# One order for attention and experts: a place for every buffer, attention scores in four row tiles, layer 1 of the first group beside attention

## The chip, the cores and the metric

One core of one Trainium2 chip. The metric is device microseconds of one execution, the median of several runs of the same program. The kernel is written by hand against the five engines: TensorE (PE), VectorE (DVE), ScalarE (ACT), GpSimd (POOL) and SyncE (SP), which issues all DMAs from one queue.

## What is computed

A chunked linear attention with decay, then two expert layers without routing, one after the other, on 3072 tokens.

```python
# attention: x (4, 8, 768, 32), a (4, 8, 768), B and C (4, 8, 768, 16); per chunk:
cum = np.cumsum(log(clip(a)), axis=-1)
L = np.exp(cum[:, :, :, None] - cum[:, :, None, :]) * causal
y = einsum('bhij,bhjd->bhid', einsum('bhin,bhjn->bhij', C, B) * L, x)
y += einsum('bhin,bhnd->bhid', C, state) * np.exp(cum)[..., None]
state = decay_full * state + sum_j B_j x_j * decay_from_j
# layer 1: (3072, 256) -> 768 -> 256
h = np.maximum(np.maximum(x @ w1, x @ w2), x @ w3);  y = h @ w_out
# layer 2: (3072, 256) -> 2048 -> 256
h = y @ w_in
P = a0 + a1*h + a2*h**2 + a3*h**3;  Q = 1 + abs(b0)*abs(h) + abs(b1)*h**2
out = (P / (Q + 1e-6)) @ w_out
```

The expert weights arrive as 64-bit floats and are converted on the chip.

## The kernel before

**Tiling.** The sequence is cut into NG = 6 groups of 128 positions of all 4 batches, so a group has T = 512 columns. A group has NU = 8 units u (a batch and a half of the 8 heads). Tensors of a unit or of a group are 128 x 512 floats; one such tile in PSUM is one of eight banks.

**Attention, per unit** (lines 585 to 642). `d_mm(u)` forms the 128 x 512 differences of the cumulated logarithms in a bank (tile `d`): two matmuls, in group 0 the second in fp32 on a tile `tl` that DVE builds. ACT takes the exponential into `e`. `s_mm(u)` forms the scores of two units at once (tile `s`): K is 64 (4 heads x 16 states), so the array holds two row tiles side by side, and the C operand `cz` is laid out block-diagonally, four heads to a unit, most of it zeros. `m_op(u)` (DVE) multiplies `s` by `e` into `m`, `y_intra(u)` multiplies by the values in four column tiles. Per group there are `y_inter` (state times C), `state` (a matmul into a `d` bank, masked and summed by DVE), `prep` (a matmul into a `d` bank, an exponential, a POOL multiplication) and `y_out` (ACT copies two banks; from group 1 on they go to DRAM, `xt_d`, and come back later as `xst`).

**Banks of attention.** `pd` holds 2 banks (`d`), `psc` 4 (`s`, two pairs), `py` 2 (`y`).

**Experts.** All expert matmuls are three fp32r passes (`mm3`, lines 768 to 770: high by high, low by high, high by low). `gy_plan(g)` is layer 1 of a group: for each of 6 slices f three blocks of 6 matmuls with ACT and DVE taking the running maximum `xa`, then the split into `hhi` (ACT) and `hlo` (POOL), then 72 matmuls into two banks: 144 x 512 columns in all. `h_plan` and `o_plan` are layer 2: per group 16 slices with 6 + 6 matmuls, and between them the rational function on ACT, DVE and POOL. In the last group `o` is a single fp32 matmul each. Layer 2 of group g is interleaved with layer 1 of group g+1; layer 1 of group 0 stands alone.

**Weights.** `plan_conv` brings in a piece (512 KB: 256 x 256 64-bit numbers) by DMA into one of 3 `wraw` buffers and converts it: two ACT operations and three DVE operations (lines 364, 367, 370) into `wa` and `we`, two POOL additions (375), an ACT copy to the high part (377 by way of 313), two POOL subtractions (379) to the low part. 28 pieces: 9 of `w1`, `w2`, `w3`, 3 of `wo1`, 8 of `win`, 8 of `wo2`.

**Order.** Each step is recorded with its engine, a cost and a due time; a planner (`Plan.emit`) finds a start for every step by list scheduling in some rounds and writes the steps out in that order, so that each engine has a fixed queue. Steps have a phase: attention is phase 0, the experts and the `wo2` pieces are phase 1, the other weight pieces have none. All of phase 0 is written before any of phase 1, and between the two `second()` closes the buffers of attention (SBUF and PSUM) and opens those of the experts, which lie on the same memory.

Of the kernel before, what the change touches and what calls it, by code (L numbers as in the profile page):

```python
# [21 lines left out]
CH = 128  # L22
# [12 lines left out]
LEAD = 3  # L35
# [10 lines left out]
class _Tile:  # L46
    def __init__(self, make, prev=None, before=None, given=None):
        self.make, self.prev, self.before, self.t = make, prev, before, given
        self.given = given is not None
        self.first, self.writers, self.readers, self.closed = -1 if self.given else None, [], [], False  # L50


class _Op:
# [3 lines left out]
    def __init__(self, i, engine, busy, fn, first, deps, after, at, phase, lock, mode, size):  # L57
        self.i, self.engine, self.busy, self.fn, self.first = i, engine, busy, fn, first
        self.deps, self.after, self.at, self.phase = deps, after, at, phase
        self.lock, self.mode, self.size = lock, mode, size  # L60
        self.plain = busy + (Plan.SWITCH if mode in ("s", "d", "ya", "st") else 0.0)
# [33 lines left out]
class Plan:  # L95
# [5 lines left out]
    ROUNDS, LOOK = 6, (0.0, 0.1, 0.2)  # L101

    def __init__(self):
        self.ops, self.rings, self.phase = [], {}, 0

    def tile(self, ring, size, make):
        ts = self.rings.setdefault(ring, [])
        t = _Tile(make, ts[-size] if len(ts) >= size else None, ts[-1] if ts else None)
        ts.append(t)
        return t  # L110

    def op(self, engine, busy, fn, reads=(), writes=(), at=None, behind=(), lock=False, mode="", size=0.0):
        i = len(self.ops)
        deps, after = set(), {w for t in behind for w in t.writers}
        for t in reads:
            assert (t.writers or t.given) and not t.closed
            deps.update(t.writers)
            t.readers.append(i)
        for t in writes:
            assert not t.closed  # L120
            if t.first is None:
                t.first = i
                if t.before and not t.before.given:
                    after.add(t.before.first)
                if t.prev:
                    t.prev.closed = True
                    deps.update(t.prev.writers + t.prev.readers)
# [5 lines left out]
                            self.phase, lock, mode, size))  # L133

    def listed(self, key, look):
# [6 lines left out]
        ready, start, end = {}, [0.0] * (n + 1), [0.0] * (n + 1)  # L142
        held = {"pool": 0.0, "dve": 0.0}
        moved, mode, landed = 0.0, "", [0.0] * self.FLIGHTS

        def at(j):
            t = self.BEGIN
            for i, _ in self.before[j]:
                if i == n or i in ops[j].after:
# [7 lines left out]
        def can(j):  # L157
            if j == n:
                start[n] = max(start[i] for i, _ in self.before[n])
                done(n)  # L160
            else:
                ready[j] = at(j)
                wait[ops[j].engine].append(j)

        def done(i):
            for j, _ in self.then[i]:
                left[j] -= 1
                if not left[j]:
                    can(j)

        for j in [j for j in range(n) if not left[j]]:
            can(j)
        for _ in range(n):
            t, e = min((max(free[e], min(ready[j] for j in w)), e) for e, w in wait.items() if w)
            j = min((j for j in wait[e] if ready[j] <= t + look), key=lambda j: (key[j], j))
            wait[e].remove(j)
            t, o = max(t, ready[j]), ops[j]
# [16 lines left out]
            done(j)  # L194
        return start, max(end)

    def placed(self, key, before, then, begin):

        n = len(before)
# [5 lines left out]
        while heap:  # L205
            _, j = heapq.heappop(heap)
            t = begin
            for i, l in before[j]:
                t = max(t, start[i] + l)
            if j < len(self.ops):  # L210
                o, last = self.ops[j], None
                while t != last:
                    last = t
                    for r in o.uses:
                        t = lines.setdefault(r, _Line()).fit(t, o.plain)
                for r in o.uses:
                    lines[r].take(t, o.plain)
# [7 lines left out]
    def emit(self, second):  # L225

        ops, n = self.ops, len(self.ops)
        self.before, self.then = [[] for _ in range(n + 1)], [[] for _ in range(n + 1)]

        def edge(i, j, l):  # L230
            self.before[j].append((i, l))
            self.then[i].append((j, l))

        for o in ops:
            for i in o.deps:
                edge(i, o.i, ops[i].lag(o))
            for i in o.after:
                edge(i, o.i, 0.0)
            if o.phase == 0:
                edge(o.i, n, 0.0)  # L240
            elif o.phase == 1:
                edge(n, o.i, 0.0)
        span = [o.plain for o in ops] + [0.0]
        back = [[(j, l - span[i] + span[j]) for j, l in self.then[i]] for i in range(n + 1)]
        key = [0.0] * (n + 1)
        for i in reversed(range(n)):
            key[i] = min([1e9 if ops[i].at is None else ops[i].at] +
                         [key[j] - l for j, l in self.then[i] if j < n])
        best = None
        for _ in range(self.ROUNDS):  # L250
            for look in self.LOOK:
                start, end = self.listed(key, look)
                if best is None or end < best[0]:
                    best = end, start
            start = best[1]
            mirror = self.placed([-(start[i] + span[i]) for i in range(n + 1)], back, self.before, 0.0)
            far = max(mirror[i] + span[i] for i in range(n + 1))
            key = [far - mirror[i] - span[i] for i in range(n + 1)]
        start = best[1]
        order = sorted(range(n), key=lambda i: (start[i], i))  # L260
        last = max(k for k, i in enumerate(order) if ops[i].phase == 0)
        early = [i for i in order[:last + 1] if ops[i].phase != 1]
        late = [i for i in order[:last + 1] if ops[i].phase == 1] + order[last + 1:]
        for part in (early, late):
            if part is late:
                second()
            for i in part:
                for t in ops[i].first:
                    t.t = t.make()
                ops[i].fn()  # L270
# [3 lines left out]
def decay_attention_max_moe_rational_moe(  # L274
# [23 lines left out]
    cvr = ctx.enter_context(tc.tile_pool(name="cvr", bufs=3))  # L298
    cva = ctx.enter_context(tc.tile_pool(name="cva", bufs=2))
    cve = ctx.enter_context(tc.tile_pool(name="cve", bufs=2))  # L300
    mp1 = ctx.enter_context(tc.tile_pool(name="mp1", bufs=1))
# [15 lines left out]
    def split(o_hi, o_lo, src, e_lo):  # L317
        copy(act, o_hi, src)
        e_lo.tensor_tensor(out=o_lo, in0=src, in1=o_hi.bitcast(F32), op=ALU.subtract)

    wsb = {}

    def w_alloc(nm, k, n, pl=wp):
        wsb[nm] = [
            pl.tile([128, k, n], F32R, name=f"{nm}_{s}") for s in ("hi", "lo")
        ]
# [3 lines left out]
    def plan_conv(plan, tok, nm, src, k0, c0):  # L330

        if nm == "wo2":
            hi, lo = (lambda i=i: wsb[nm, k0 // 2][i] for i in range(2))
        else:
            hi, lo = (lambda i=i: wsb[nm][i][:, k0:k0 + 2, c0:c0 + 256] for i in range(2))
        shape = [128, 2, 256]
        wide = src.dtype != F32
        raw = plan.tile("wraw", 3, lambda: cvr.tile(shape + [2], U32, tag="wraw", name="wraw") if wide
                        else cvr.tile(shape, F32, tag="wraw", name="wst"))
        rows = slice(128 * k0, 128 * k0 + 256)  # L340
        if not wide:
            plan.op("dma", 0.4, lambda: nc.sync.dma_start(
                out=raw.t, in_=src[rows, c0:c0 + 256].rearrange("(k p) n -> p k n", p=128)), [], [raw], size=262.0)
            plan.op("act", 0.53, lambda: copy(act, hi(), raw.t), [raw], [tok])
            plan.op("pool", 1.26, lambda: pool.tensor_tensor(out=lo(), in0=raw.t, in1=hi().bitcast(F32),
                                                             op=ALU.subtract), [raw], [tok])
            return
        a = plan.tile("wa", 2, lambda: cva.tile(shape, U32, tag="wa", name="wa"))
        e = plan.tile("we", 2, lambda: cve.tile(shape, U32, tag="we", name="we"))
        af = lambda: a.t.bitcast(F32)  # L350
        low, high = (lambda: raw.t[:, :, :, 0]), (lambda: raw.t[:, :, :, 1])
        raws[0] += 1
        first = f"w{raws[0]}" in FIRST
# [4 lines left out]
        plan.op("dma", 0.42, lambda: nc.sync.dma_start(  # L358
            out=raw.t.rearrange("p k n t -> p k (n t)"),
            in_=src.bitcast(U32)[rows, 2 * c0:2 * c0 + 512].rearrange("(k p) n -> p k n", p=128)), [], [raw],  # L360
            FIRST.index(f"w{raws[0]}") - 1000.0 if first else 6.0 + PIECE * raws[0],
# [725 lines left out]
```

## Time and profile before

| | us |
|---|---|
| median of 3 runs (lowest to highest) | 576.49 (576.09 to 577.17) |
| the profiled execution | 576.76 |
| its span, first to last instruction | 575.0 |
| busy: PE / DVE / ACT / POOL | 555.9 / 512.4 / 439.6 / 439.9 |

A profile is one execution. Matmuls are pipelined: a matmul of 512 columns is shown as 389 ns, while the next starts 225 ns after it, so rates are read from start to start, not from the mean. Waits are inferred; the engine named is the one whose event came last.

### The profile page before, as it was taken

What the parts mean: (1) busy time and instruction counts of PE and PEld (TensorE: products, weight loads), DVE (VectorE), ACT (ScalarE), POOL (GpSimd) and SP (SyncE); (2) the same over time, 40 slices, a digit from 0 to 9 for tenths busy, and PEclk for the clock granted to TensorE, in tenths of its full rate; (3) what the DMA queues carried; (4) which work ended last, traced back from release to release, by engine and by line L of the source; (5) the groups of instructions that cost most, each with busy time, mean ns of one, the idle gap of its engine ahead of it and who ended that gap; (6) DMA issues with size and microseconds to landing.
All of it is one profiled execution on the core that took longest, in us unless ns stands there. A gap on an engine that the chain in (4) does not pass through costs nothing.

```text
span 575.0 us, 8132 instructions
## 1 busy us (share of the span) xinstructions
PE 555.9 (97%) x2758; PEld 410.0 (71%) x2758; DVE 512.4 (89%) x777; ACT 439.6 (76%) x756; POOL 439.9 (77%) x410
## 2 busy tenths in 40 slices
PE   8998889899999999999999999999999999999997
PEld 3333333678788888888888888888888888887563
DVE  7998978689999998889888988898898888988996
ACT  5787767576888878787878787878777868688993
POOL 1787767798999777768587877676866999869883
PEclk9999999999999999999999999999999999999999
DMA  7878873542000100101000000000000010001000
GB/s 213 265 213 303 261 223 112 198 132 73 1 0 2 33 5 0 38 1 38 0 1 36 1 20 19 0 26 12 1 1 2 0 38 0 1 1 38 1 0 36
DMA packets 19044, 33.70 MB, mean 59 GB/s; under 512 B 3523, under 2 KB 4027, under 8 KB 19003
## 3 DMA queue, kind: packets, MB, share of 16 engines
q1 hardware_dynamic: 19003, 33.20, 18.1%
q8 instruction: 21, 0.34, 0.2%
q14 instruction: 20, 0.16, 0.1%
HBM read 27.27 MB, written 5.91 MB: 58 GB/s over the span
## 4 chain that ended last, share of the span: by engine, by line
PE 70%; DVE 11%; POOL 9%; DMA 4%; ACT 3%; issue 2%; SPq 1%; POOLq 0%; ACTq 0%; DVEq 0%
PE pg L768 9%; PE pg L770 9%; PE pg L769 9%; PE ph L770 6%; PE ph L769 6%; PE ph L768 6%; PE po L770 6%; PE po L769 6%; PE po L768 6%; DVE m L627 2%; PE s L594 2%; DVE wa L370 2%; PE po L990 1%; POOL wa L375 1%; DVE wa L364 1%
## 5 line engine op out<-in xcount | busy, mean ns | idle before, releaser
L972 POOL TENSOR_TENSOR glo<-w,ghi 128x512 fp32r<-128x512 f32 x80 | 106.3, 1329 | 21.6 <-ACT ghi L313 21.3
L768 PE MATMUL pg<-xhi,w_hi 128*128 128x512 f32 x202 | 79.3, 392 | 1.7 <-DVE xa L851 1.4
L769 PE MATMUL pg<-xlo,w_hi 128*128 128x512 f32 x202 | 78.6, 389 | 0.0
L770 PE MATMUL pg<-xhi,w_lo 128*128 128x512 f32 x202 | 78.6, 389 | 0.0
L959 ACT ACTIVATE pr<-v,qc 128x512 f32<-128x512 f32 x83 | 57.4, 692 | 18.7 <-POOL v L938 11.5
L313 ACT ACTIVATE ghi<-w 128x512 fp32r<-128x512 f32 x80 | 50.5, 631 | 23.3 <-PE po L770 20.0
L412 POOL TENSOR_TENSOR hlo<-xa,hhi 128x512 fp32r<-128x512 f32 x36 | 49.7, 1383 | 20.5 <-ACT hhi L313 20.5
L770 PE MATMUL ph<-yhi,win_lo 128*128 128x512 f32 x160 | 62.2, 389 | 0.0
L768 PE MATMUL ph<-yhi,win_hi 128*128 128x512 f32 x160 | 62.2, 389 | 0.0
L769 PE MATMUL ph<-ylo,win_hi 128*128 128x512 f32 x160 | 62.2, 389 | 0.0
L768 PE MATMUL po<-ghi,wo_hi 128*128 128x512 f32 x160 | 62.2, 389 | 0.0
L769 PE MATMUL po<-glo,wo_hi 128*128 128x512 f32 x160 | 62.2, 389 | 0.0
L770 PE MATMUL po<-ghi,wo_lo 128*128 128x512 f32 x160 | 62.2, 389 | 0.0
L964 DVE SCALAR_TENSOR_TENSOR pr<-w,co,pr 128x512 f32<-128x512 f32 x83 | 62.1, 749 | 0.0
L938 POOL TENSOR_TENSOR v<-t,v 128x512 f32<-128x512 f32 x44 | 57.2, 1299 | 3.6
L961 DVE SCALAR_TENSOR_TENSOR v<-v,pr 128x512 f32<-128x512 f32 x83 | 56.4, 680 | 3.6 <-ACT pr L960 3.2
L375 POOL TENSOR_TENSOR wa<-wa,we 128x256 uint32<-128x256 uint32 x56 | 44.8, 814 | 19.1 <-DVE wa L370 17.7
L966 DVE SCALAR_TENSOR_TENSOR w<-v,pr 128x512 f32<-128x512 f32 x83 | 56.7, 684 | 1.8
L960 ACT ACTIVATE pr<-pr 128x512 f32<-128x512 f32 x86 | 50.2, 584 | 1.6
L851 DVE TENSOR_TENSOR xa<-xa,pg 128x512 f32<-128x512 f32 x67 | 45.6, 681 | 4.4 <-PE ph L770 2.1
L768 PEld LDWEIGHTS pg<-xhi,w_hi 128*128 128x128 f32 x202 | 37.9, 188 | 11.5 <-DVE xa L851 2.2
L956 POOL TENSOR_TENSOR w<-w,t 128x512 f32<-128x512 f32 x20 | 25.9, 1296 | 24.3 <-DVE v L945 22.2
(167 smaller groups left out, 1475.2 us busy)
## 6 DMA issues: line engine op xcount, KB each, us to landing
wraw<-in_wo_dram SPq DMA_DIRECT2D x11, 512.0 KB
wraw<-in_w_dram SPq DMA_DIRECT2D x9, 512.0 KB
wraw<-in_win_dram SPq DMA_DIRECT2D x8, 512.0 KB
xn<-in_xn_dram SPq DMA_DIRECT2D x6, 512.0 KB
out_dram<-ob SPq DMA_DIRECT2D x12, 256.0 KB
xt_d<-xo SPq DMA_DIRECT2D x10, 256.0 KB
xst<-xt_d SPq DMA_DIRECT2D x10, 256.0 KB
bt<-in_bz_dram SPq DMA_DIRECT2D x6, 256.0 KB
```

Source lines behind the costliest of these rows:

```text
L313: act.activation(out=o, in_=i, func=AF.Copy)
L375: plan.op("pool", 0.7, lambda k=k: pool.tensor_tensor(out=a.t[:, k], in0=a.t[:, k], in1=e.t[:, k], op=ALU.add), [e], [a])
L768: pe.matmul(dst, wh, hi, start=first, stop=False)
L769: pe.matmul(dst, wh, lo, start=False, stop=False)
L770: pe.matmul(dst, wl, hi, start=False, stop=last)
L938: pop(1.26, lambda: pool.tensor_tensor(out=f(v), in0=f(t1), in1=f(v), op=ALU.mult), [t1], [v])
L959: aop(0.6, lambda: act.activation(out=f(r), in_=f(v), func=AF.Ln, bias=qc), [v], [r])
L960: aop(0.49, lambda: act.activation(out=f(r), in_=f(r), func=AF.Exp, scale=-1.0), [], [r])
L961: dop(0.6, lambda: dve.scalar_tensor_tensor(out=f(v), in0=f(v), scalar=QC, in1=f(r), op0=ALU.add, op1=ALU.mult), [r], [v])
L964: dop(0.67, lambda: dve.scalar_tensor_tensor(out=f(r), in0=f(w), scalar=c(0), in1=f(r), op0=ALU.add, op1=ALU.mult), [w], [r])
L966: dop(0.6, lambda: dve.scalar_tensor_tensor(out=f(w), in0=f(v), scalar=2.0, in1=f(r), op0=ALU.subtract, op1=ALU.mult), [v, r], [w])
L972: pop(1.26, lambda: pool.tensor_tensor(out=f(lo), in0=f(w), in1=f(hi).bitcast(F32), op=ALU.subtract), [w, hi], [lo])
```

## The change

- **One plan.** The phases and `second()` are gone, and with them the rule that all of attention is written before any expert step. The planner gets one more choice (`KEEP`: prefer a PE step of the same tiling mode for up to 1.5 us), 8 rounds instead of 6.
- **A place for each buffer.** Instead of pools that are closed and opened there is one SBUF pool and one PSUM pool in which each tile names its place, and a tile waits for the last tile of that place, whatever it was. The eight banks are S0 to S3, D, G, Y0, Y1. Attention: scores in S0 to S3, `y` in Y0 and Y1, and `d`, `prep` and `state` all in D (in group 0 alone every other `d` is in G). Experts: `pg` = G, D; `ph` = S0, S1; `pr` = Y0, Y1; sums in S2, S3. Layer 1 of group 0 (18 + 2 banks, `EARLY` = 20) uses G alone. The eight `wo2` weight pairs lie where `cz`, `lr`, `xn` and `xo` of attention lay.
- **Scores as four row tiles.** K is 32 (2 heads x 16 states); one `s_mm` now does half a group: two batches x four row tiles, each 256 columns, into four banks. `cz` is half as large. Heads are regrouped accordingly in the host layout of B, C and `a`. There are 12 `s_mm` instead of 24, and each needs all four S banks free of the one before.
- **Coarser steps.** `y_intra` does two units in one step (24 steps instead of 48), `y_inter` all batches in one, `y_out` writes one 512 KB transfer, and `x_plan` reads one.
- **Layer 1 of group 0** can lie beside attention; its six `hlo` subtractions go to DVE instead of POOL.
- **Weights on the host** are laid out so that each piece is one run of 4 KB per partition (two of 2 KB before).

```diff
-    ROUNDS, LOOK = 6, (0.0, 0.1, 0.2)
+    ROUNDS, LOOK, KEEP = 8, (0.0, 0.1, 0.2), (0.0, 1.5)
-    def tile(self, ring, size, make):
-        ts = self.rings.setdefault(ring, [])
-        t = _Tile(make, ts[-size] if len(ts) >= size else None, ts[-1] if ts else None)
+    def tile(self, place, make):
+        t = _Tile(make, self.last.get(place, ()))
+        self.last[place] = [t]
         return t
...
-        early = [i for i in order[:last + 1] if ops[i].phase != 1]
-        late = [i for i in order[:last + 1] if ops[i].phase == 1] + order[last + 1:]
-        for part in (early, late):
-            if part is late:
-                second()
+        for i in best[1]:
...
-    cz = [sp.tile([128, 4, T], F32, name=f"cz{i}") for i in range(2)]
+    cz = [sl.tile([128, 2, T], F32, tag=f"L{i}", name=f"cz{i}") for i in range(2)]
...
-    def s_mm(u):
-        s_t[u], s_t[u + 1] = ts = new("psc", "s", 4), new("psc", "s", 4)
+    def s_mm(k):
+        ts = [bank(f"S{h}") for h in range(4)]
         def mm():
-            for q, t in enumerate(ts):
-                r = slice(64 * q, 64 * q + 64)
-                pe.matmul(t.t.rearrange("p (f i) -> p f i", f=4), btg[g].t[r, c], cz[g % 2][r, :, c],
-                          start=True, stop=True)
+            for b in range(2):
+                c = slice(CH * (2 * a + b), CH * (2 * a + b) + CH)
+                for h, t in enumerate(ts):
+                    r = slice(32 * h, 32 * h + 32)
+                    pe.matmul(t.t.rearrange("p (h b i) -> p h b i", h=2, b=2)[:, :, b], btg[g].t[r, c],
+                              cz[g % 2][r, :, c], start=(b == 0), stop=True, skip_group_check=True)
...
     def d_mm(u):
-        t = new("pd", "d", 2)
+        t = bank("G" if g < PAIR and d_n[0] % 2 else "D")
...
     def state(g):
-        t = new("pd", "d", 2)
+        t = bank("D")
...
+    for k in range(F2 // 2):
+        wsb["wo2", k] = new(f"L{(0, 1, 6, 7, 2, 3, 4, 5)[k]}", (128, 2, 2, DM), F32R)
...
+    pg, ph, pr = (ring(p, bank) for p in (["G", "D"], ["S0", "S1"], ["Y0", "Y1"]))
     def gy_bank(g):
-        if g == 0 and banks[0] % 5 > 2:
-            return new("ph", "ph", 2)
-        return new("pg", "pg", 2)
+        if g:
+            return pg()
+        return bank("G") if banks[0] <= EARLY else late()
...
-            psplit(of(xa), hi, lo, "pool")
+            psplit(of(xa), hi, lo, "pool" if g else "dve")
```

## Rows read from the trace of the kernel before

**Rows 1.** Windows: stretch, length, busy of each engine (instructions), granted clock, DMA share, GB/s

```profile
0.00:10.00 10.00, 7.71 (x25) 3.21 (x25) 7.74 (x16) 5.36 (x10) 2.04 (x6) 1.00 0.65 188
10.00:103.60 93.60, 82.71 (x741) 33.96 (x739) 83.89 (x139) 66.88 (x121) 66.27 (x79) 0.98 0.72 224
103.60:139.60 36.00, 34.93 (x155) 28.04 (x152) 29.17 (x37) 22.45 (x40) 30.93 (x34) 1.00 0.48 161
139.60:215.40 75.80, 75.17 (x330) 61.59 (x329) 73.57 (x108) 62.54 (x108) 64.38 (x58) 1.00 0.03 8
215.40:291.20 75.80, 75.80 (x336) 62.77 (x335) 67.97 (x104) 59.82 (x102) 55.62 (x47) 1.00 0.04 14
```

**Rows 2.** Timeline of PE in attention: start, length, engine, line, operation, count

```profile
65.02 1.13 PE L594 MATMUL s<-cz,bt 64*128 64x512 f32 x4
66.08 1.09 PE L673 MATMUL d<-xn,bn 128*64 128x128 f32 x16
67.11 0.39 PE L605 MATMUL d<-trib 128*128 128x512 bf16 x1
67.33 0.38 PE L607 MATMUL d<-lr 128*128 128x512 bf16 x1
67.64 0.43 PE L638 MATMUL y<-m,xn 128*32 128x128 f32 x8
68.00 1.16 PE L649 MATMUL y<-ct,st 64*128 64x128 f32 x16
69.09 0.42 PE L638 MATMUL y<-m,xn 128*32 128x128 f32 x8
```

**Rows 3.** Timeline where attention ends: the first expert steps of ACT and DVE

```profile
107.44 0.60 ACT L313 ACTIVATE xa<-pg 128x512 f32<-128x512 f32 x1 [2.11 <-DMA xt_d<-xo]
108.07 0.69 DVE L851 TENSOR_TENSOR xa<-xa,pg 128x512 f32<-128x512 f32 x1 [2.10 <-PE ph L770]
```

**Rows 4.** DVE by line, 0 to 103.6 us: busy, mean ns, idle before

```profile
L627 DVE TENSOR_TENSOR m<-s,e 128x512 f32<-128x512 f32 x48 | 30.6, 680 | 2.3 <-PE s L594 2.2
L370 DVE SCALAR_TENSOR_TENSOR wa<-wraw,wa 128x512 uint32<-128x512 uint32 x19 | 18.2, 958 | 0.7
L364 DVE TENSOR_SCALAR wa<-wa 128x512 f32<-128x512 f32 x19 | 11.3, 594 | 5.6 <-ACT wa L363 5.5
L367 DVE TENSOR_SCALAR wa<-wa 128x512 uint32<-128x512 uint32 x19 | 11.3, 593 | 0.7
...
L691 DVE SCALAR_TENSOR_TENSOR st<-st,e,d 128x128 f32<-128x128 f32 x16 | 4.5, 344 | 0.1
...
L684 DVE TENSOR_TENSOR d<-d,co_raw 128x512 f32<-128x512 f32 x4 | 2.8, 688 | 0.0
L485 DVE MEMSET cz<- 128x1024 f32 x2 | 1.8, 912 | 0.4 <-issue 0.4
```

**Rows 5.** DVE by line, 103.6 to 139.6 us

```profile
L370 DVE SCALAR_TENSOR_TENSOR wa<-wraw,wa 128x512 uint32<-128x512 uint32 x7 | 8.2, 1169 | 0.2
L364 DVE TENSOR_SCALAR wa<-wa 128x512 f32<-128x512 f32 x7 | 5.8, 828 | 3.6 <-ACT wa L363 3.6
L367 DVE TENSOR_SCALAR wa<-wa 128x512 uint32<-128x512 uint32 x7 | 5.2, 744 | 0.2
L412 DVE TENSOR_TENSOR ylo<-ph,yhi 128x512 fp32r<-128x512 f32 x1 | 0.7, 692 | 0.7 <-ACT yhi L313 0.7
```

**Rows 6.** Timeline, 80 to 86 us: a state update, then one `d` bank's round

```profile
80.14 1.09 PE L673 MATMUL d<-xn,bn 128*64 128x128 f32 x16
83.75 0.39 PE L605 MATMUL d<-trib 128*128 128x512 bf16 x1 [2.16 <-DVE st L691]
83.98 0.38 PE L607 MATMUL d<-lr 128*128 128x512 bf16 x1
84.45 0.60 ACT L622 ACTIVATE e<-d 128x512 f32<-128x512 f32 x1 [3.60 <-PE d L607]
```

More of the change, by code (lines that the diff above doesn't have):

```diff
@@ L115, in op @@
         for t in reads:
-            assert (t.writers or t.given) and not t.closed
+            assert t.writers and not t.closed
             deps.update(t.writers)
@@ L122, in op @@
                 t.first = i
[L123 to L127, printed above, removed]
+                for p in t.prevs:
+                    p.closed = True
+                    deps.update(p.writers + p.readers)
             deps.update(t.writers + t.readers)
@@ L155, in at @@
             return t
[L157 to L162, printed above, removed]
-                wait[ops[j].engine].append(j)
[L165 to L172, printed above, removed]
+        for j in range(n):
+            if not left[j]:
+                ready[j] = self.BEGIN
+                wait[ops[j].engine].append(j)
         for _ in range(n):
             t, e = min((max(free[e], min(ready[j] for j in w)), e) for e, w in wait.items() if w)
-            j = min((j for j in wait[e] if ready[j] <= t + look), key=lambda j: (key[j], j))
+            j = min((j for j in wait[e] if ready[j] <= t + look),
+                    key=lambda j: (key[j] - (keep if e == "pe" and ops[j].mode == mode else 0.0), j))
             wait[e].remove(j)
+            order.append(j)
             t, o = max(t, ready[j]), ops[j]
@@ L193, in listed, with placed @@
             start[j], free[e] = t, t + o.busy
[L194 to L199, printed above, removed]
+            for i, _ in self.then[j]:
+                left[i] -= 1
+                if not left[i]:
+                    ready[i] = at(i)
+                    wait[ops[i].engine].append(i)
+        return order, start, max(end)
+    def placed(self, key, before, then):
+        ops, n = self.ops, len(self.ops)
         left = [len(b) for b in before]
@@ L206, in placed @@
             _, j = heapq.heappop(heap)
[L207 to L215, printed above, removed]
+            t, last, o = max([start[i] + l for i, l in before[j]], default=0.0), None, ops[j]
+            t = max(t, 0.0)
+            while t != last:
+                last = t
                 for r in o.uses:
-                    lines[r].take(t, o.plain)
+                    t = lines.setdefault(r, _Line()).fit(t, o.plain)
+            for r in o.uses:
+                lines[r].take(t, o.plain)
             start[j] = t
@@ L251, in emit @@
             for look in self.LOOK:
[L252 to L261, printed above, removed]
-        early = [i for i in order[:last + 1] if ops[i].phase != 1]
-        late = [i for i in order[:last + 1] if ops[i].phase == 1] + order[last + 1:]
-        for part in (early, late):
-            if part is late:
-                second()
[L267 to L270, printed above, removed]
+                for keep in self.KEEP:
+                    order, start, end = self.listed(key, look, keep)
+                    if best is None or end < best[0]:
+                        best = end, order, start
+            start = best[2]
+            mirror = self.placed([-(start[i] + span[i]) for i in range(n)], back, self.before)
+            far = max(mirror[i] + span[i] for i in range(n))
+            key = [far - mirror[i] - span[i] for i in range(n)]
+        start = best[2]
+        for i in best[1]:
+            for t in ops[i].first:
+                t.t = t.make()
+            ops[i].fn()
 @with_exitstack
@@ L347, in plan_conv @@
             return
-        a = plan.tile("wa", 2, lambda: cva.tile(shape, U32, tag="wa", name="wa"))
-        e = plan.tile("we", 2, lambda: cve.tile(shape, U32, tag="we", name="we"))
+        raw = new(f"R{n % 3}", [128, 2, 256, 2], U32)
+        a, e = new(f"C{n % 2}", shape, U32), new(f"E{n % 2}", shape, U32)
         af = lambda: a.t.bitcast(F32)
         low, high = (lambda: raw.t[:, :, :, 0]), (lambda: raw.t[:, :, :, 1])
[L352 to L361, printed above, removed]
-            behind=[cum_t] if raws[0] < 4 and not first else (), size=525.0)
@@ L418, in of, with part @@
         return f
+    def part(t, k):
+        f = lambda: t.t[:, k]
+        f.tile = t
+        return f
     when = {}
@@ new lines, in y_inter, with mm, y_out @@
+    def y_inter(g):
+        def mm():
+            for b in range(NB):
+                c = slice(CH * b, CH * b + CH)
+                for q in range(2):
+                    r = slice(64 * q, 64 * q + 64)
+                    pe.matmul(y_t[g, q].t[:, c], st[g].t[r, c], ctg[g].t[r, c],
+                              start=False, stop=True, skip_group_check=True)
+        op("pe", 0.89, mm, [st[g], ctg[g]], [y_t[g, 0], y_t[g, 1]], when["yi", g], mode="r2")
+    def y_out(g):
+        xo = xo_r((128, KD, T))
+        for q in range(2):
+            op("act", 0.5, lambda q=q: copy(act, xo.t[:, q], y_t[g, q].t), [y_t[g, q]], [xo])
+        if g:
+            xt_t[g] = mark()
+            load(lambda: xt_d[g], lambda: xo.t, [xt_t[g]], [xo], kb=524)
+        else:
+            for q in range(2):
+                hi, lo = new(f"xhi{q}", (128, T), F32R), new(f"xlo{q}", (128, T), F32R)
+                psplit(part(xo, q), hi, lo, "dve")
+                x0.append((hi, lo))
@@ L1020, in decay_attention_max_moe_rational_moe @@
                 o_plan(s, h_plan(s))
-    plan.emit(second)
+    plan.emit()
 def layout(inputs):
```

442 lines of the change are left out of this document (214 added, 228 removed).

## Prediction, made before the change was run

> **What bounds the kernel now.** I first read the table of windows, one row for each stage [rows 1]. The stages are: start (to 10 us), attention (to 103.6), layer 1 of group 0 alone (to 139.6), then one stretch of 75.8 us for each group. In the stretches the reader is to see 336 matmuls in 75.8 us, 225.6 ns from start to start, with PE busy all the time; DVE has 68.0 us of work there, 90%. In the first such stretch DVE already has 73.6 of 75.8 us, 97%, and PE has lost only 0.6 us: so 97% is a load that DVE can carry here. Ahead of the stretches it is different. In attention PE is busy for 82.7 and DVE for 83.9 of 93.6 us: neither is full, each waits for the other in turn. In the 36.0 us of layer 1 alone DVE has 29.2 and POOL 30.9, mostly weight conversion. The change works only on the stages ahead of 215.4 us; what follows (five stretches and the end) has the same matmuls, the same number of buffers and the same banks to each kind, and I leave it as it is. So the question is when the first stretch will end, against 215.4 us now.
>
> **The change on PE.** The prices are read from start to start in a piece of attention without gaps [rows 2]: a score step 1.06 us, a state step 1.03, a `d` pair 0.53, a unit of `y_intra` 0.36, the whole of `y_inter` 1.09.
> - Scores: 24 steps become 12. A step keeps its length if four row tiles run side by side, since each tile streams 2 x 256 columns as it streamed 512 before. No row shows four row tiles; the nearest is `y_intra`, whose four column tiles get through 8 instructions in 0.36 us. I take 1.06, a gain of 12 x 1.06 = 12.7 us; the other end is 2.12, no gain.
> - `y_intra` and `y_inter` have the same columns in fewer steps; fewer changes of the tiling mode save something between 0 and 24 x 0.36 = 8.6 us. I take 0, because the expert blocks that now lie between bring changes of their own, at a like price (20 blocks, 0 to 7 us).
> - Layer 1 of group 0: 144 x 0.2256 = 32.5 us, no longer alone.
>
> PE then has 82.7 - 12.7 + 32.5 = 102.5 us from 10 us on, and could begin layer 2 at 112.5 instead of 139.6.
>
> **The end of the barrier.** At the end of attention the first ACT step of the experts waits 2.1 us for the last transfer out of `xo`, and DVE 2.1 us behind it [rows 3]. Both are part of the 36.0 us, of which 32.5 are matmuls: 3.5 us at most go with the barrier. They are in the sum already, since there layer 1 stands at 32.5.
>
> **The change on DVE.** Nothing is taken off DVE but one `cz` memset of 0.9 us [rows 4]. Six `hlo` subtractions come over from POOL; one like it, `ylo`, takes 0.69 us [rows 5]: 4.1 us. So up to the beginning of layer 2 DVE has 7.7 + 83.9 + 29.2 [rows 1] - 0.9 + 4.1 = 124.0 us of work, if all that is done by then now is done by then afterwards. It is not: six of the seven conversions between 103.6 and 139.6 us are `wo2` pieces, at (8.2 + 5.8 + 5.2) / 7 = 2.74 us of DVE each [rows 5], and their targets now lie on buffers that attention uses to its end (`cz`, `lr`, `xn`, `xo`). Only the first few can be converted before that; I take three and move three, 8.2 us, into the first stretch. How many it is hardly matters: what leaves one stage lengthens the other.
>
> The first 10 us hold 7.7 of the remaining 115.8; for the other 108.1 the load of DVE decides. Lower end: 90%, as in attention now. Upper end: 97%, as in the first stretch. I take 95%, nearer to the upper, because PE has 102.5 us of work where DVE has 108.1 and can run ahead of it, which it cannot now. Layer 2 then begins at 10 + 108.1 / 0.95 = 123.8 us, later than the 112.5 that PE would allow. The first stretch has 73.6 + 8.2 = 81.8 us of DVE; at 97% it lasts 84.3 us instead of 75.8. It ends at 208.1 us: 7.3 us earlier. With 97% in both it is 205.7 (9.7 earlier), with 90% 214.4 (1.0 earlier).
>
> What is late next is therefore DVE, and the halved scores are worth less than their 12.7 us: of the 27 us that PE could gain, DVE lets 16 through and takes 8.5 back in the first stretch.
>
> **The other engines and the queues.** ACT has 5.4 + 66.9 + 22.5 = 94.8 us up to 139.6, POOL 99.2 [rows 1], less 6 `hlo`; neither fills 124 us. The SP queue loses 12 of the `cz` issues, 5 of `xt_d` and 5 of `xst`; the bytes stay. The weights in runs of 4 KB may arrive sooner; DMA is at 0.72 in attention [rows 1], I count nothing, and a gain of a microsecond or two is in the range.
>
> **What is added as a wait.** All `d` banks but those of group 0 are now one, D, where there were two, and a score step needs all four S banks, where one pair could be filled while the other was read. Behind a `d` step that waits for D stand, in PE's fixed queue, score steps, `y` steps and blocks of layer 1; behind them ACT's exponentials and DVE's products. One round of the bank is the pair of matmuls and the exponential: from 83.75 to 85.05, 1.30 us [rows 6]. Forty rounds are 52 us; five of `prep` at about 1.1 (an estimate: the same without the second matmul) 5.5; four states at 1.03 [rows 2] + 0.69 + 4 x 0.34 [rows 4] = 3.1, up to the 3.6 that one holds its bank now (80.14 to 83.75 [rows 6]), 13; four rounds of group 0 at some 2 us, 8. Together 79 us, so attention could not end before 89 us if nothing ever stood in a round's way. That leaves 123.8 - 89 = 35 us for 57 rounds, 0.6 us each, before this chain is later than DVE. I count nothing for it, but the cover is thin.
>
> Here a page of the Trainium skill speaks against the change: "TensorEngine Tiling (Array Packing)", section Restrictions and Gotchas, says that row tiling increases PSUM pressure, since different row tiles have to write different banks. That is what is seen in the diff: four row tiles take four of the eight banks at once, and the second `d` bank is what had to go. The rule gives no price; by it the sum would be that of the second rival below, and no run so far shows which it is.
>
> **The rivals.**
> 1. *DVE gets faster too.* In attention a conversion takes DVE (18.2 + 11.3 + 11.3) / 19 = 2.15 us [rows 4], in layer 1 alone 2.74 [rows 5], where POOL is busier. If six pieces come down to 2.15 (3.5 us) and DVE has no gaps, the first stretch ends at 10 + 108.1 + 81.8 - 3.5 = 196 us. That would be 557; halfway to the forecast is 563. For it: POOL loses the `hlo`. Against it: no stage yet ran above 97%.
> 2. *The bank D becomes the bound; slower than before.* If 18 rounds wait for a block of layer 1 (6 x 0.2256 = 1.35 us) and the other 39 for one ACT step of 0.6 us [rows 6], that is 48 us, and attention ends at 137. DVE, starved of `e`, loses that time, and the first stretch, still with `wo2`, ends at 137 + 84 = 221: 5.6 us later, 582. It turns slower from 0.74 us a round (attention ending at 131). For it: PE is dense with blocks that cannot be interrupted, and a state keeps D through two DVE steps, which wait in a full queue. Against it: `e` has four buffers, and DVE has conversions to do meanwhile.
> 3. *The row tiles don't run side by side.* The 12.7 us stay on PE: it would need until 125.2, and with gaps as now (88%) until 140. Together with the longer first stretch that ends near 215: 575 to 577, no change.
>
> **How the numbers follow.** The profiled execution took 576.76 us, 1.76 more than its span, and 0.27 more than the median. 576.76 - 7.3 = 569.5, by the median 569.2. Forecast: 569.2 us, its own range 564 to 575. Chances: forecast 0.55, rival 1 0.14, rival 2 0.22, rival 3 0.09. A measurement of this kernel can tell about 0.2% (1.2 us). Faster: 0.69; same: 0.09; slower: 0.22. The range reaches half into rival 1 and to rival 2's price: 560 to 583.
>
> **What would show it.** Right: 12 score steps of about 1.06 us; layer 2 beginning near 124 us; DVE at 95% up to there; a first stretch of some 84 us with `wo2` conversions in it; 75.8 us for each later one. Wrong: DVE under 92% before layer 2 with PE waiting for exponentials or for the state's DVE steps (rival 2); score steps of 2 us (rival 3); conversions below 2.15 us (rival 1); later stretches longer than 75.8 us, which no step here foresees.

## The result and the profile after

| | before | after |
|---|---|---|
| median, us (lowest to highest) | 576.29 (575.53 to 577.17) | 569.5 (569.31 to 570.01) |
| ratio, 95% interval | | 0.9883 (0.9866 to 0.99) |
| span of the profiled execution, us | 575.0 | 568.2 |

The forecast was 569.2 us. The windows of the kernel after, cut where its layer 2 begins and then as in [rows 1] (length, busy of PE, its weight loads, DVE, ACT, POOL, granted clock, DMA share, GB/s):

```profile
0.00:10.00 10.00, 8.78 (x26) 4.40 (x27) 7.24 (x16) 5.66 (x9) 1.16 (x5) 1.00 0.72 230
10.00:124.70 114.70, 103.97 (x970) 62.05 (x979) 104.66 (x171) 83.31 (x149) 81.13 (x95) 1.00 0.64 210
124.70:208.60 83.90, 81.00 (x357) 65.89 (x354) 82.17 (x122) 71.05 (x125) 76.37 (x68) 1.00 0.10 34
208.60:284.40 75.80, 75.80 (x336) 62.78 (x335) 68.13 (x101) 57.46 (x100) 57.25 (x48) 1.00 0.05 14
284.40:360.20 75.80, 74.75 (x329) 61.24 (x328) 66.16 (x98) 57.27 (x99) 54.45 (x45) 1.00 0.04 15
360.20:436.00 75.80, 74.18 (x327) 60.73 (x326) 67.93 (x101) 57.85 (x100) 55.39 (x46) 1.00 0.02 7
```

Attention and layer 1 of group 0 now share one stage, and layer 2 begins at 124.7 us instead of 139.6 [rows 1]. In the 114.7 us before it PE is busy for 104.0 and DVE for 104.7, 91% each. In the next 83.9 us DVE has 82.2 of work, 98%.

The timeline of PE shows what a score step costs, and how close the parts of attention and layer 1 lie (start, length, line, count):

```profile
11.06 1.15 PE L597 MATMUL S<-cz,A 32*128 32x256 f32 x16
12.14 1.09 PE L677 MATMUL D<-L,A 128*64 128x128 f32 x16
...
31.33 1.15 PE L597 MATMUL S<-cz,A 32*128 32x256 f32 x16
32.41 0.64 PE L642 MATMUL Y<-A,L 128*32 128x128 f32 x16
32.98 0.50 PE L749 MATMUL G<-xhi,w_hi 128*128 128x512 f32 x1
33.31 0.39 PE L750 MATMUL G<-xlo,w_hi 128*128 128x512 f32 x1
33.55 0.40 PE L751 MATMUL G<-xhi,w_lo 128*128 128x512 f32 x1
```

A score step takes 1.08 us from start to start, as one took before (1.06 [rows 2]), and does twice as much: the four row tiles do run side by side. Two units of `y_intra` in one step take 0.57 us instead of 2 x 0.36.

DVE by line up to layer 2, in the kernel after (busy, mean ns, idle before):

```profile
L630 DVE TENSOR_TENSOR A<-S,A 128x512 f32<-128x512 f32 x48 | 32.1, 683 | 2.6 <-ACT A L625 2.2 <-PE S L597 0.3
L334 DVE SCALAR_TENSOR_TENSOR C<-R,C 128x512 uint32<-128x512 uint32 x23 | 20.5, 892 | 0.7
L328 DVE TENSOR_SCALAR C<-C 128x512 f32<-128x512 f32 x24 | 13.4, 558 | 4.1 <-ACT C L327 4.0
L331 DVE TENSOR_SCALAR C<-C 128x512 uint32<-128x512 uint32 x24 | 13.1, 546 | 0.7
...
L386 DVE TENSOR_TENSOR H<-X,H 128x512 fp32r<-128x512 f32 x6 | 6.6, 1096 | 1.6 <-ACT H L286 1.4
```

23 of 28 conversions are done by then, so three of the eight `wo2` pieces. They cost DVE 0.89 + 0.56 + 0.55 = 2.0 us each (2.15 in [rows 4], 2.74 in [rows 5]), while an `hlo` takes 1.10 us, not 0.69.

Not all of the lead lasts. The DMAs that write the output of a group are issued at these times, in the kernel before and in the kernel after (timeline of SP; the rows of groups 0 and 1):

```profile
233.89 1.67 SPq L1003 DMA_DIRECT2D out_dram<-ob  x2
...
309.62 1.58 SPq L1003 DMA_DIRECT2D out_dram<-ob  x2
```

```profile
223.19 1.61 SPq L992 DMA_DIRECT2D out_dram<-A  x2
...
300.00 3.36 SPq L992 DMA_DIRECT2D out_dram<-A  x2
```

Group 0 comes out 10.7 us earlier, the groups after it 9.6, 7.4, 6.5, 8.1 and 6.8, and the end of the span 6.8. In the windows above PE misses 1.05 and 1.62 us in two later stretches. In the kernel before it missed none in the same two:

```profile
291.20:367.00 75.80, 75.80 (x336) 62.78 (x335) 66.94 (x101) 60.17 (x102) 54.99 (x46) 1.00 0.04 15
367.00:442.80 75.80, 75.80 (x336) 62.74 (x336) 66.51 (x102) 60.53 (x101) 54.73 (x47) 1.00 0.02 8
```

The one wait that the PE lines of the kernel after show there (284.4 to 436 us), 2.7 us in four pieces, is for DVE's running maximum (`xa`, here `X`), which has to read bank D first:

```profile
L749 PE MATMUL D<-xhi,w_hi 128*128 128x512 f32 x34 | 13.7, 402 | 2.7 <-DVE X L840 2.7
```

### The profile page after: what moved, and what is told of

The parts are those of the page before. It is cut to its first block, busy times and chain, and to the rows that moved or that the text cites. A ratio compares the mean times of both kernels' runs of the same rounds, so it can differ in the third digit from the quotient of the medians.

```text
span 568.2 us, 8235 instructions
## 1 busy us (share of the span) xinstructions
PE 546.7 (96%) x2844; PEld 411.8 (72%) x2854; DVE 513.7 (90%) x782; ACT 433.6 (76%) x756; POOL 437.9 (77%) x403
## 4 chain that ended last, share of the span: by engine, by line
PE 42%; DVE 32%; POOL 12%; ACT 7%; issue 5%; DMA 1%; SPq 0%; POOLq 0%; DVEq 0%; ACTq 0%
PE S L750 6%; PE S L751 6%; PE S L749 6%; PE S L979 4%; PE G L749 4%; DVE X L840 4%; DVE Y L953 4%; PE G L751 3%; PE G L750 3%; DVE A L950 3%; DVE A L955 3%; PE D L749 3%; PE D L751 3%; PE D L750 3%; DVE A L630 2%
## 5 line engine op out<-in xcount | busy, mean ns | idle before, releaser
L961 POOL TENSOR_TENSOR A<-A,A 128x512 fp32r<-128x512 f32 x80 | 106.9, 1337 | 10.6 <-ACT A L286 10.3
L948 ACT ACTIVATE Y<-A,qc 128x512 f32<-128x512 f32 x83 | 57.7, 695 | 45.4 <-POOL A L927 30.0
L950 DVE SCALAR_TENSOR_TENSOR A<-A,Y 128x512 f32<-128x512 f32 x83 | 56.4, 680 | 8.2 <-ACT Y L949 7.9
L749 PE MATMUL S<-A,L 128*128 128x512 f32 x160 | 62.3, 389 | 0.0
L750 PE MATMUL S<-A,L 128*128 128x512 f32 x160 | 62.3, 389 | 0.0
L751 PE MATMUL S<-A,L 128*128 128x512 f32 x160 | 62.3, 389 | 0.0
L953 DVE SCALAR_TENSOR_TENSOR Y<-A,co,Y 128x512 f32<-128x512 f32 x83 | 62.1, 748 | 0.0
L927 POOL TENSOR_TENSOR A<-A,A 128x512 f32<-128x512 f32 x44 | 57.8, 1314 | 3.6
L955 DVE SCALAR_TENSOR_TENSOR A<-A,Y 128x512 f32<-128x512 f32 x83 | 56.7, 683 | 1.3
L286 ACT ACTIVATE A<-A 128x512 fp32r<-128x512 f32 x80 | 50.4, 630 | 8.8 <-DVE A L955 7.4
L749 PE MATMUL G<-xhi,w_hi 128*128 128x512 f32 x126 | 51.7, 410 | 4.1 <-ACT X L286 2.0
L949 ACT ACTIVATE Y<-Y 128x512 f32<-128x512 f32 x86 | 50.3, 584 | 1.8
L945 POOL TENSOR_TENSOR A<-A,A 128x512 f32<-128x512 f32 x20 | 26.1, 1307 | 21.6 <-DVE A L934 19.7
L750 PE MATMUL S<-K,win_hi 128*128 128x512 f32 x96 | 37.5, 390 | 0.4 <-DVE K L386 0.4
L749 PE MATMUL S<-K,win_hi 128*128 128x512 f32 x96 | 37.5, 390 | 0.0
```

The source lines that it names most:

```text
L286: act.activation(out=o, in_=i, func=AF.Copy)
L749: pe.matmul(dst, wh, hi, start=first, stop=False)
L750: pe.matmul(dst, wh, lo, start=False, stop=False)
L751: pe.matmul(dst, wl, hi, start=False, stop=last)
L927: pop(1.26, lambda: pool.tensor_tensor(out=f(v), in0=f(t1), in1=f(v), op=ALU.mult), [t1], [v])
L948: aop(0.6, lambda: act.activation(out=f(r), in_=f(v), func=AF.Ln, bias=qc), [v], [r])
```

## Experiments

Each kernel is the one after (once the one before) with the edit shown. Ratios are to the kernel before, measured beside it on the same chip. From one set of runs to the next its median was 576.2 to 577.1 us, so a difference of less than 1 us between two medians of the table says nothing. Except in e1 to e4 and e11, which keep the order of the steps, the planner finds an order of its own for each kernel.

| run | edit | median, us | ratio (95%) |
|---|---|---|---|
| after | | 569.5 | 0.9883 (0.9866 to 0.99) |
| e1 | clamp cut short | 564.37 | 0.9793 (0.9774 to 0.9812) |
| e2 | the same in the kernel before | 570.98 | 0.9911 (0.9886 to 0.9937) |
| e3 | clamp twice | 588.42 | 1.0209 (1.0176 to 1.0243) |
| e4 | scores twice | 576.71 | 1.0008 (0.9997 to 1.0019) |
| e5 | layer 1 behind attention | 581.37 | 1.0089 (1.0045 to 1.0133) |
| e6 | the same, two `d` banks | 576.15 | 0.9997 (0.9984 to 1.001) |
| e7 | `hlo` on POOL | 567.25 | 0.9844 (0.9829 to 0.9859) |
| e8 | other forms in group 0 | 570.07 | 0.9892 (0.987 to 0.9914) |
| e9 | without KEEP | 572.43 | 0.9935 (0.9918 to 0.9951) |
| e11 | exponentials in halves | 569.27 | 0.9866 (0.9844 to 0.9888) |
| e12 | e7, four `tl` on POOL | 571.85 | 0.9903 (0.9874 to 0.9931) |
| e13 | e7, two `d` banks in two groups | 569.14 | 0.9866 (0.984 to 0.9893) |

### What bounds the time up to layer 2: e1 to e4

```diff
 e1, e2
-            out=af(), in0=af(), scalar1=F64_LOW, scalar2=F64_HIGH, op0=ALU.max, op1=ALU.min), [], [a], lock=True)
+            out=af()[:, 0:1, 0:4], in0=af()[:, 0:1, 0:4], scalar1=F64_LOW, ..., op1=ALU.min), [], [a], lock=True)
 e3
+            for _ in range(2):
+                dve.tensor_scalar(out=af(), in0=af(), scalar1=F64_LOW, scalar2=F64_HIGH, op0=ALU.max, op1=ALU.min)
 e4 (s_mm)
-            for b in range(2):
+            for b in (0, 1, 0, 1):
```

> The changed kernel with one DVE operation of each of the 28 weight conversions (the clamp of the magnitude) cut from 512 columns to 4; the planner's costs, and so the order of the steps, are as in the changed kernel. The computation leaves out the clamp of very small and very large weights. It takes some 28 x 0.5 = 14 us off DVE and nothing off PE. Theory 'DVE bounds the time up to the end of the first stretch': layer 2 begins 8 to 10 us earlier (then PE, with 104 us of work, becomes the bound), the first stretch is about 2 us shorter, in all 10 to 13 us: 557 to 560 us. Rival 'the one bank D bounds attention': DVE was not waited for, 3 us at most: 566 us or more.

> The same cut of the clamp in the kernel before (the clamp of very small and very large weights is left out). Theory: there PE and DVE wait for each other in turn and layer 1 of group 0 stands alone, so the 14 us taken off DVE are worth less: 4 to 8 us, 568 to 572 us. If DVE was as much the bound before as after, 10 to 13 us: 563 to 566 us. If PE alone was the bound before, nothing: 576 us.

> The changed kernel with the clamp done twice in each of the 28 conversions, in the same order of steps: 28 x 0.59 = 16.6 us more on DVE. Theory 'DVE bounds': nearly all of it shows, 14 to 18 us: 584 to 588 us. Rival 'bank D bounds': there is room for at least half of it, 8 us or less: 578 us or less.

> The changed kernel with the matmuls of each of the 12 score steps done twice, in the same order of steps: 12 x 1.07 = 12.8 us more on PE, about what the four row tiles took off. Theory 'DVE bounds, PE has some room': PE had 104 us of work in the 114.7 us between 10 us and layer 2, so about 2 us of 12.8 show at least, and about 8 with gaps as now: 572 to 578 us. If PE is the bound: 582 us. If the halved scores are worth nothing by now: 570 us.

Measured: e1 5.1 us less, e2 5.3 less than before, e3 18.9 more, e4 7.2 more. The windows of e1, e3 and e4, up to layer 2 and after it:

```profile
10.00:120.37 110.37, 102.31 (x970) 62.04 (x979) 94.49 (x172) 82.89 (x149) 79.76 (x95) 1.00 0.65 219
120.37:202.70 82.33, 80.42 (x354) 65.49 (x351) 80.50 (x120) 70.63 (x125) 75.17 (x67) 1.00 0.10 34
```

```profile
10.00:139.80 129.80, 110.91 (x971) 65.30 (x979) 116.27 (x193) 83.61 (x148) 79.13 (x95) 0.95 0.57 186
139.80:227.00 87.20, 81.66 (x358) 66.10 (x355) 86.06 (x127) 71.70 (x126) 75.56 (x67) 1.00 0.10 33
```

```profile
10.00:131.66 121.66, 112.88 (x1162) 71.99 (x1170) 101.14 (x171) 83.28 (x149) 78.50 (x95) 1.00 0.59 198
131.66:215.40 83.74, 80.75 (x356) 65.73 (x353) 81.94 (x121) 70.94 (x125) 76.11 (x67) 1.00 0.10 33
```

More work on DVE shows in full: in e3 15.5 us of it over the two windows put layer 2 off by 15.1 us and make the next stretch 3.3 us longer. The granted clock also falls, to 0.95 up to layer 2, and the four runs of e3 lie between 586.56 us (mean clock 0.991) and 589.81 (0.982). So what e3 takes beyond the added work can be the clock; that was not separated.

Less work shows in part: in e1 DVE has 10.2 us less ahead of layer 2, and layer 2 begins 4.3 us earlier. So the expectation for e1 missed, and so did its rival (566 us or more): DVE is the bound, but other limits stand 4 us behind it and not 8 to 10. PE is then busy for 102.3 of 110.4 us (93%), and of the 8.1 us that it misses, 4.7 are waits in front of a step in bank D, until ACT has read the bank (total, times, longest):

```profile
PE D L610 <- ACT A L625: 3.4, 5, 0.7
PE D L677 <- ACT A L575: 0.7, 1, 0.7
PE D L572 <- ACT A L625: 0.6, 2, 0.4
```

e4 says the same from the other side. Its expectation put 12.8 us more on PE. The trace shows less, since a doubled step takes 1.94 us from start to start instead of 1.08:

```profile
32.60 2.01 PE L597 MATMUL S<-cz,A 32*128 32x256 f32 x32
34.54 0.65 PE L642 MATMUL Y<-A,L 128*32 128x128 f32 x16
```

That is 12 x 0.86 = 10.3 us; 7.0 of them show ahead of layer 2 and nothing after it, so PE had some 3 us of room, close to the 4 of e1. By the same share the 12.4 us that the change takes off the score steps (24 x 1.06 - 12 x 1.08) are worth some 8 us in this kernel. This is an estimate: the halving was not tried alone.

e2 fits its expectation: in the kernel before, too, part of DVE's work was on the path.

### Layer 1 beside attention, and the one bank D: e5, e6, e11

```diff
 e5, e6
-EARLY = 20
+EARLY = 0
 e6
-PAIR = 1
+PAIR = 6
 e11
-        op("act", 0.5, lambda: act.activation(out=e.t, in_=t.t, func=AF.Exp), [t], [e])
+            for k in range(2):
+                act.activation(out=e.t[:, 256 * k:256 * k + 256], in_=t.t[:, 256 * k:256 * k + 256], func=AF.Exp)
```

> The changed kernel with EARLY = 0: layer 1 of group 0 takes its banks in turn from S0, D, S1 and G, which attention uses to its end, so it stands behind attention again; one d bank as in the changed kernel. Theory 'what pays is PE work of layer 1 in the gaps of attention, as far as DVE lets it': attention ends near 104 us as before, layer 2 begins at 138 to 141, the wo2 conversions fall beside layer 1 again and the first stretch is back at 76 to 77 us: 573 to 577 us, most of the gain gone. If the halved scores alone carry the gain, it stays below 571. If the one bank D bounds attention when layer 1 is not in the way, attention ends beyond 110 us: 580 us or more.

> As e5, and every other d of all groups in bank G (PAIR = 6), so that attention has two d banks as before the change. Against e5 this is the price of the one bank D. Theory (little): 0 to 3 us below e5. Rival (bank D bounds attention): 5 us or more below e5.

> The changed kernel with each of the 48 exponentials of attention done as two halves of 256 columns, in the same order of steps. By 0.594 us for 512 columns and 0.38 to 0.42 us for the 256-column copies of the start, a pair takes some 0.2 us longer, and so does each round of bank D: 45 rounds in D, 9 us on its chain; ACT gets 9 us more work and stays under 85% up to layer 2. If bank D bounds attention with layer 1 beside it, 7 to 9 us more: 577 to 579 us. If it has the room that the prediction gave it (0.6 us a round), 0 to 2 us: 569.5 to 572 us. Between: D and DVE share the waiting, 3 to 5 us.

Measured: e5 11.9 us more than the kernel after, and slower than the kernel before by its whole interval; e6 5.2 us below e5, the same as the kernel before; e11 no change. So for e5 the last of its three cases came true: the last `y_intra` of attention starts at 112.1 us, and layer 2 at 144.7. With layer 1 behind attention the measured time shows nothing of the halved scores, the coarser steps and the missing barrier. This is not a clean zero: e6 also has the six `hlo` on DVE, and its runs have a mean clock of 0.984 to 0.991 where those of the kernel before have 0.994 to 1.000. By the slope over its own ten runs, some 0.3 us for each 0.001, e6 would be about 3 us faster than the kernel before at the same clock (an estimate). One bank D instead of two costs 5.2 us, the rival that I had given little; the clock does not explain it, as the runs of e5 and e6 with 0.988 are 5.5 us apart (582.15 and 576.64). The `d` lines of PE show the wait, first of the kernel after (whole span), then of e5 and e6 (10 to 112 us; count, busy, mean, idle before and for whom):

```profile
L610 PE MATMUL D<-sm 128*128 128x512 bf16 x44 | 17.2, 390 | 4.1 <-ACT A L625 3.4 <-DVE A L694 0.3
```

```profile
L610 PE MATMUL D<-sm 128*128 128x512 bf16 x42 | 17.3, 413 | 15.0 <-ACT A L625 9.7 <-DVE A L694 4.1 <-ACT A L575 0.7
```

```profile
L610 PE MATMUL D<-sm 128*128 128x512 bf16 x22 | 9.3, 421 | 6.1 <-ACT A L625 3.6 <-DVE A L694 2.5
L610 PE MATMUL G<-sm 128*128 128x512 bf16 x23 | 9.1, 395 | 3.4 <-ACT A L625 3.4
```

In e5 PE stands idle for 15.0 us before `d` steps, waiting until ACT has read the bank or DVE has updated the state; with two banks for 9.5; in the kernel after for 4.1, though it has one bank: there the blocks of layer 1 fill the same gaps. e11 makes each exponential two of 0.381 us instead of one of 0.593, so 0.17 us longer (lines of ACT, of the kernel after and of e11, 10 to 124 us):

```profile
L625 ACT ACTIVATE A<-D 128x512 f32<-128x512 f32 x43 | 25.5, 593 | 9.2 <-PE D L612 6.2 <-PE Y L653 1.8 <-remote 0.5
L628 ACT ACTIVATE A<-D 128x256 f32<-128x256 f32 x86 | 28.1, 381 | 8.5 <-PE D L612 8.1
```

Nothing else becomes longer, up to layer 2 and after it:

```profile
10.00:124.17 114.17, 104.37 (x980) 62.12 (x979) 103.54 (x171) 85.72 (x195) 81.17 (x95) 1.00 0.64 211
124.17:207.90 83.73, 80.82 (x356) 65.72 (x353) 81.96 (x122) 70.78 (x125) 76.15 (x67) 1.00 0.10 34
```

So with layer 1 beside attention, and DVE as loaded as here, the chain of D has about 44 x 0.17 = 7.5 us of room. e1 shows what stands behind this room: with less work on DVE the waits for D are most of what PE still misses. The page "TensorEngine Tiling (Array Packing)" of the Trainium skill warns in its section Restrictions and Gotchas that row tiling raises PSUM pressure. The trace agrees, and the runs give a price: 5.2 us for the bank given up, as long as nothing else fills the waits, and nothing that could be measured when something does (e11, and e13 below with a second bank in one group more).

### Where DVE could be relieved: e7, e8, e12, e13

```diff
 e7, e12, e13
-            psplit(of(xa), hi, lo, "pool" if g else "dve")
+            psplit(of(xa), hi, lo, "pool")
 e8
-        kind = HL[k % len(HL)] if last else HV[k % len(HV)]
+        kind = HL[k % len(HL)] if last else ("HAHA" if g == 0 else HV)[k % len(HV)]
 e12 (tl of group 0)
+            e_tl = "pool" if u % 2 else "dve"
...
 e13
-PAIR = 1
+PAIR = 2
```

> The changed kernel with the six hlo subtractions of layer 1 of group 0 on POOL, as before the change: DVE loses 6.6 us up to layer 2, POOL gains some 9 (81 of 114.7 us busy now). From e1, in which 12 us less DVE work ahead of layer 2 gave 4.3 us, I expect 2 us less: 567 to 569 us. If the longer way over POOL holds up layer 1: 570 to 573 us.

> The changed kernel with the rational function of group 0 in the forms H, A, H, A instead of H, A, H, P: in four slices of the first stretch one DVE operation of 0.69 us goes, for one of ACT, and a POOL operation of 1.3 us comes in place of one of 0.88. Theory 'DVE at 98% is the bound of the first stretch' (83.9 us long where PE needs 75.8): 2 to 3 us less, 566.5 to 568 us. If POOL (76 of 83.9 us) is as much a bound there: no change, 569 to 570 us.

> As e7 (hlo of group 0 on POOL), and four of the eight tl operations of group 0 on POOL, which is nearly idle in the first 20 us (4.5 us busy) while DVE is at 72 to 93%: 3 us less on DVE there. Theory (DVE and PE both near full up to layer 2): 1 us below e7, 566 to 567 us. If the slower tl hold up the first d steps: 568 us or more.

> As e7, and two d banks in the first two groups instead of the first alone (PAIR = 2); layer 1 of group 0 can then begin only after group 1 has left bank G, at about 40 us instead of 27. If D holds up attention: 1 to 3 us below e7, 564 to 566 us. If layer 1 on its one bank, begun later, ends later than attention: 570 us or more.

Measured: e7 2.2 us below the kernel after, and clear of it, as expected; e7 is the fastest kernel here that does the whole work. e8 is not clear of the kernel after, so its rival case came true. e12 is not clear of the kernel after either, but it was meant to be faster than e7 and is clearly slower (ratios 0.9903 and 0.9844, intervals apart). That is the second case of its expectation, and nothing more was tried on it. e13 is clear of neither the kernel after nor e7, and fits neither of its cases. In e7 only a third of the 6.6 us shows, and up to layer 2 DVE's busy time hardly falls (104.7 to 104.1 us; over both stages 186.8 to 183.3), as the window and the lines of e7 up to layer 2 say:

```profile
10.00:123.26 113.26, 103.53 (x981) 61.20 (x979) 104.14 (x163) 81.46 (x147) 85.71 (x100) 1.00 0.64 209
...
L334 DVE SCALAR_TENSOR_TENSOR C<-R,C 128x512 uint32<-128x512 uint32 x23 | 21.1, 916 | 0.7
L328 DVE TENSOR_SCALAR C<-C 128x512 f32<-128x512 f32 x23 | 15.6, 677 | 4.0 <-ACT C L327 4.0
L331 DVE TENSOR_SCALAR C<-C 128x512 uint32<-128x512 uint32 x23 | 14.6, 635 | 0.6
```

With six more subtractions on POOL the two `TENSOR_SCALAR` steps of a conversion take 677 and 635 ns instead of 558 and 546: 4.8 us come back that way. That POOL is the reason is not shown: in e5 the same steps take 673 and 624 ns (10 to 125 us), with POOL busy for 66% of the time up to layer 2, against 71% in the kernel after. The windows of e8 and e13, up to layer 2 and after it:

```profile
10.00:131.43 121.43, 106.99 (x994) 64.50 (x993) 110.06 (x179) 87.18 (x157) 85.59 (x99) 1.00 0.66 211
131.43:209.20 77.77, 76.79 (x338) 63.03 (x337) 74.15 (x111) 68.91 (x121) 70.05 (x64) 1.00 0.05 17
```

```profile
10.00:117.71 107.71, 102.28 (x947) 60.74 (x947) 97.03 (x156) 77.43 (x138) 77.56 (x89) 0.98 0.62 205
117.71:209.30 91.59, 82.20 (x377) 65.69 (x376) 88.53 (x126) 75.18 (x130) 84.78 (x78) 0.98 0.15 52
```

Layer 2 begins at 131.4, 124.7 or 117.7 us in three kernels (e8, after, e13) whose profiled executions have spans within 1 us of each other. The sum of DVE's work over both windows is 184.2, 186.8 and 185.6 us of 199.2, 198.6 and 199.3: where the planner puts a conversion moves the border between the stages, not the end. DVE is busy for 92 to 94% of the two stages in these three, for 95% in e9 and for 91 and 89% in e1 and e4, so no fixed ceiling of DVE is shown. In e8 it has 2.6 us less work than in the kernel after, and the time did not follow; which of the other engines holds it back was not separated.

### The planner's new choice: e9

```diff
-    ROUNDS, LOOK, KEEP = 8, (0.0, 0.1, 0.2), (0.0, 1.5)
+    ROUNDS, LOOK, KEEP = 8, (0.0, 0.1, 0.2), (0.0,)
```

> The changed kernel without the planner's new choice (KEEP = 0 alone: no preference for a PE step of the tiling mode that is set). Every later entry into another tiling mode costs PE about 0.1 us; with layer 1 beside attention PE has little to spare up to layer 2 (104 of 114.7 us). If the choice mattered: 1 to 3 us more, 570.5 to 572.5 us. If DVE hides it, or the planner's best order was found without it: 569 to 570 us.

Measured: 2.9 us more, so the choice carries some 40% of the gain; the intervals are apart. It comes with a different order of all steps, so this is the price of that order and not of the mode changes alone. DVE has 190.3 us of work over the two stages there, 3.4 more than in the kernel after, which alone would be enough for the 2.9.

## Why the prediction was right, and where it was not

**PE.** 102.5 us of work from 10 us on were predicted, 104.0 measured; the score step at 1.06, measured 1.08. Rival 3 (row tiles one after the other) falls. (Its 215 us was loosely added: 125.2 to 140 and a first stretch of 84.3 give 209.5 to 224.) `y_intra` did gain, 0.15 us in each of 24 steps, counted at nothing. The blocks of layer 1 cost some of that: the first matmul of a block takes 0.33 us from start to start (32.98 to 33.31 above), the next 0.24. The 144 matmuls of layer 1 are 108 and then 36, not 72 as the description of the kernel has it; the sum used 144.

**DVE up to layer 2.** The begin was predicted at 123.8 and is 124.7, but with two errors that cancel: the load is 91%, not 95%, and the work 104.7 us, not 108.1. Conversions became cheaper by some 5 us (2.0 each), and the six `hlo` cost 2.5 us more than the 4.1 counted. The row that they were priced by, `ylo`, reads a bank; the `xlo` of the same trace has both inputs in SBUF, as `hlo` has, and its median was 0.93 us (0.68 to 1.51). The lower end of the range, 90%, was the nearer row. e1 and e4 show why: PE at 91% and bank D are only 3 to 4 us behind, so neither engine runs as full as DVE does in the stretches.

**The first stretch.** By the windows it was to be 84.3 us with 81.8 of DVE, and 83.9 with 82.2 are seen; three `wo2` pieces ahead of it, as taken. But those windows are laid from the end of the span. By the output DMAs, group 0 is 10.7 us early, not 7.3, so only 14.9 - 10.7 = 4.2 us of the lead were lost there, not 8.5. And 1.35 of the 4.2 were no loss: when layer 2 began in the kernel before, PE had done six matmuls of layer 1 of group 1 already, in the kernel after none. Nor is DVE alone what PE waits for in this stretch: its lines show 1.4 us for DVE and 1.5 us for ACT, which copies a bank of layer 1.

**The later stretches.** Here a step failed: "I leave it as it is". Another 3.9 us are lost between the output of group 0 and the end, with 2.7 us of PE waiting for the running maximum on DVE. The two losses make up the 8.1 us between layer 2's lead (14.9) and the end's (6.8), where 8.5 were predicted. Every kernel of the new plan has such gaps (74.2 to 75.6 us of PE in two or three stretches of 75.8), neither kernel of the old plan does. The cause is open: the order in the stretches, the single `x` buffer of both halves (`L8`), and the places of the banks of layer 1 all differ, and none was tried alone.

**Bank D.** I counted nothing and wrote that the cover is thin; the cover was the room behind DVE. In the kernel after that holds (e11). Without layer 1 beside attention it is gone, and the chain costs 5.2 us (e5 against e6). So rival 2 names a real mechanism that this change pays for and hides at once. (The rounds that the prediction lists are 40 + 5 + 4 + 4 = 53, not 57; the room is then 0.66 us a round instead of 0.6, and the argument is the same.)

**The signs, the other engines and the range.** Of the signs listed for being wrong, three came: DVE under 92% before layer 2 (91%) with PE waiting 3.4 us for exponentials, conversions below 2.15 us, and later stretches that are longer. The first did not mean that bank D was the bound (e11). Rival 1 (DVE faster by less POOL beside it) appears in small, with conversions at 2.0 us; but POOL is busy for 71% of the stage as it was for 71% of attention before [rows 1], so its reason is not shown. The end, 569.5, lies 0.3 us from the forecast, inside every range given. That closeness is luck: terms of 3 to 4 us cancelled twice.

## What to carry to other kernels

Work moved into the gaps of another stage pays as far as the next full engine lets it: add up each engine's work over all the stages that are merged, not PE's alone. An edit that frees one resource by taking another (four row tiles for a bank) should be priced with and without the work that fills the wait; here the second bank is worth nothing measurable beside layer 1, and 5.2 us without it, where the halved scores, the coarser steps and the missing barrier left the time as it was. And a time that comes out right is no proof of the terms: look at milestones in between, such as the output of each group.

## What the runs showed of the hardware that was not expected

PE's granted clock falls where attention has no other work in its gaps. Windows of e5 in attention, then of e6:

```profile
10.00:60.00 50.00, 41.77 (x416) 22.54 (x416) 42.67 (x72) 33.50 (x59) 28.76 (x34) 0.88 0.77 246
60.00:110.00 50.00, 38.34 (x413) 19.46 (x415) 41.73 (x68) 35.88 (x64) 36.46 (x46) 0.92 0.56 188
```

```profile
10.00:60.00 50.00, 40.77 (x397) 20.62 (x399) 46.78 (x77) 33.21 (x62) 35.53 (x40) 0.83 0.76 252
60.00:110.00 50.00, 45.38 (x498) 27.41 (x491) 44.34 (x73) 39.77 (x73) 38.05 (x47) 1.00 0.61 204
```

In e5, where PE waits 15 us for bank D, the mean clock is 0.88 and 0.92. As the clock has two levels, 1.2 and 2.4 GHz, PE then spends about a fifth of this time at 1.2 GHz (an estimate). The bank is not the whole reason: e6 has two banks, and its clock is 0.83 in the first 50 us and 1.00 in the next. In the kernel after it stays at 2.4 GHz throughout, and in the kernel before it falls a little in attention (0.98 [rows 1]). The clock differs from run to run of one kernel, and the time with it: e5 took 577.88 us in a run with a mean clock of 1.000 and 586.36 in one with 0.980. The run at full clock lies 8.4 us above the kernel after, where the median lies 11.9 above it: the rest goes with the clock. The Trainium skill's "TensorE: Matmul & The Clock Gate", section Part 1: The HAM clock gate (the "warmup" mystery), says that throttled is the default state and activity releases it; the rows agree as far as they go: with the gaps of attention filled the clock stayed up, and where PE had to wait longer for DVE (e3) it fell to 0.95.
